# The Fourier half of an attention + FNet kernel: sequence transform first with stored operand pieces, feature transform second

## The chip, the cores and the metric

One core of one Trainium2 chip runs the whole program; the other cores are idle. The metric is the device time of one execution in microseconds (us); the time of a kernel is the median of its runs. Engines: PE (TensorE, matmuls), DVE (VectorE), ACT (ScalarE), POOL (GpSimd) and SP (SyncE, which here issues nearly all DMA transfers).

## What is computed

Two independent halves with S = 2048 rows, D = 1024 columns, all in float32. Half A is full attention with 32 heads of width 32 and an output projection; half B mixes x with Fourier matrices along both axes and keeps the real part. The two outputs stand side by side.

```python
def _A_ref(x, wqkv, wo):
    B, S, D = x.shape
    H = 32; Dh = D // H
    qkv = (x @ wqkv).reshape(B, S, 3, H, Dh).transpose(2, 0, 3, 1, 4)
    q, k, v = qkv[0], qkv[1], qkv[2]
    p = softmax(einsum("bhqd,bhkd->bhqk", q, k) * Dh ** -0.5)
    o = einsum("bhqk,bhkd->bhqd", p, v)
    return o.transpose(0, 2, 1, 3).reshape(B, S, D) @ wo

def _B_ref(x, dft_seq_re, dft_seq_im, dft_hid_re, dft_hid_im):
    a = einsum("bsd,ed->bse", x, dft_hid_re)
    b = einsum("bsd,ed->bse", x, dft_hid_im)
    y = einsum("ts,bse->bte", dft_seq_re, a) - einsum("ts,bse->bte", dft_seq_im, b)
    return y
```

The real part is therefore Cr x Wr' - Ci x Wi', with C the sequence matrices (2048 x 2048) and W the feature matrices (1024 x 1024). The products may be taken from either side.

## The kernel before

**Matmuls.** Every dense product (qkv, the two Fourier steps, the projection) is done to more than the precision of one pass: an operand piece is a raw float32 tile that is split into a rounded high half and a low half (raw minus high), and each 128x128 by 128x512 chunk costs three matmuls, high·high, low·high and high·low (`group`, L404). Each such product also goes through one level of a seven-multiplication scheme: seven products of sums of quadrants in place of eight (`ORDER`), so that operands are often sums of two or three quadrants, and results are gathered from several products (`gather`, L950 to L982). What is stationary is called a piece (four chunks, tiles `h` and `l`, rings HR and LR of four each); what is moving lies in slots (`moving`, one slot holds both halves).

**Making an operand.** `fetch` loads a raw quadrant (L453, tile `raw`, a ring of six), loads a second one if there is a sum (L462, tile `g`), adds them on POOL or DVE (L469) and stores sums that are needed again (L478). `halves` casts the high half on DVE (L491) or on ACT (L489, where `spare` allows it) and subtracts the low half on POOL or DVE (L494). SP issues in its own order; a transfer whose ring place is not yet free holds back all that follow.

**Attention.** Three streams: S, the scores (L1278, tile `psS`, pairs of matmuls), whose row maxima DVE takes (L1284) and whose exponentials' sums ACT takes (L1287); T, the transposed scores with the maxima as two extra rows of `qs` (L1400, tile `psT`), exponentials by ACT into `pt` (L1404); V, the product with v (L1419, batches of 20, 20 and 24 matmuls a quarter wide). Before the first T of a head the maxima go from DVE to DRAM (L1325, `m_d`) and come back into `qs` (L1326). A head's result is scaled by `rt` (L1448) and stored to `o_d` (L1450). 

**Order of the work.** A planner in the program (`Plan`) imitates the engines with assumed costs and writes a fixed order for PE, ACT, DVE, POOL and SP. The chunks of the dense products are a list of fills in program order: qkv, `dense1`, `dense2`, `project`. The planner starts a fill where no attention matmul is ready or where fills are behind their share of the attention work; so the two Fourier steps lie between the matmuls of the heads. `rank` sets which of the ready operations of an engine goes first. After the last head come the rest of the Fourier fills and then the projection, which reads `o_d` and the weights `wo`: its slots 20 to 27 are gated by all stores of `o_d` (`behind`), its raw tiles are a ring of six of their own, and its products run in the order 1, 7, 2, 6, 5, 3, 4, 96 matmuls each.

**Fourier half before.** `dense1` multiplies x (stationary pieces, from `xb`) by the two feature matrices at once (moving, from `wd`): 7 products x 16 groups of 4 chunks, results to DRAM (`ab_d`). `dense2` multiplies pieces of the sequence matrices (stationary, from `ct`) with `ab_d` (moving): for each of two halves m of the inner dimension 7 products x 8 groups of 8 chunks, the first half's results to `y_d` and added at the end of the second (tile `c`).

Of the kernel before, what the change touches and what calls it, by code (L numbers as in the profile page):

```python
# [220 lines left out]
def kernel(  # L221
# [26 lines left out]
    ab_d = [[[dram.tile([P, NB], F32, name=f"ab_d{m}_{e}_{k}") for k in range(NS)] for e in range(2)] for m in range(2)]  # L248

    s1_d = [[dram.tile([P, 4, P], F32, name=f"s1_d{x}_{i}") for i in range(8)] for x in (5, 6)]  # L250
    t1_d = [[dram.tile([P, NB], F32, name=f"t1_d{x}_{n}") for n in range(8)] for x in (5, 6)]
# [5 lines left out]
    u3_d = [[dram.tile([P, NB], F32, name=f"u3_d{i}_{m}") for m in range(2)] for i in range(8)]  # L257
    s2_d = [[[dram.tile([P, 4, P], F32, name=f"s2_d{x}_{i}_{k}") for k in range(4)] for i in range(8)] for x in (5, 6)]
    t2_d = [[[dram.tile([P, NB], F32, name=f"t2_d{x}_{m}_{k}") for k in range(8)] for m in range(2)] for x in (5, 6)]
    y_d = [[dram.tile([P, NB], F32, name=f"y_d{i}_{e}") for e in range(2)] for i in range(NS)]  # L260
# [83 lines left out]

    MM, PV, SWITCH, TINY = 0.2275, 0.853, 0.40, 0.17
# [16 lines left out]
    FILL = 3 * (7 * 24 * 4 + 7 * 16 * 4 + 7 * 8 * 16 + 2 * 8 * 4)  # L362
# [559 lines left out]
    ORDER = (1, 2, 5, 6, 7, 3, 4)  # L922

# [6 lines left out]

    def gather(what, X, Y, u3, to, wrote, part=None, split=False):

# [13 lines left out]
        def finish(ps, last):  # L946
# [63 lines left out]
            if what in (2, 3):  # L1010
                return put(X.at, [X.users], X.last, ALU.add, to, wrote, part)
            if Y is None:
                return put(lambda: got["c"], [cusers], cload, ALU.subtract, to, wrote, part)
            return put(Y.at, [Y.users], Y.last, ALU.subtract, to, wrote, part)
# [3 lines left out]
    ab_st = [[[[] for _ in range(NS)] for _ in range(2)] for _ in range(2)]  # L1018

    def dense1():  # L1020
        s1, t1 = ({5: [[] for _ in range(8)], 6: [[] for _ in range(8)]} for _ in range(2))
        u3 = [[[], []] for _ in range(8)]

        def a_terms(p, i):
            q = lambda r, k: xb[8 * r + i, :, 4 * k : 4 * k + 4, :]
            return {
                1: [(1, q(0, 0), [])], 2: [(1, q(0, 1), [])], 4: [(1, q(1, 1), [])],
                5: [(1, q(1, 0), []), (1, q(1, 1), [])],
                6: [(1, s1_d[0][i], s1[5][i]), (-1, q(0, 0), [])],
                7: [(1, q(0, 0), []), (-1, q(1, 0), [])],  # L1030
                3: [(1, q(0, 1), []), (-1, s1_d[1][i], s1[6][i])],
            }[p]

        def b_terms(p, n):
            m, c = divmod(n, 4)
            q = lambda k, e: wd[m, 4 * k + c, :, e * NB : e * NB + NB]
            return {
                1: [(1, q(0, 0), [])], 2: [(1, q(1, 0), [])], 3: [(1, q(1, 1), [])],
                5: [(1, q(0, 1), []), (-1, q(0, 0), [])],
                6: [(1, q(1, 1), []), (-1, t1_d[0][n], t1[5][n])],  # L1040
                7: [(1, q(1, 1), []), (-1, q(0, 1), [])],
                4: [(1, t1_d[1][n], t1[6][n]), (-1, q(1, 0), [])],
            }[p]

        def load_b(x, n):
            p = ORDER[x]
            B[x][n] = moving((8 * x + n) % 12, b_terms(p, n), (t1_d[p - 5][n], t1[p][n]) if p in (5, 6) else None)

        B = [[None] * 8 for _ in ORDER]
        for n in range(4):  # L1050
            load_b(0, n)
        X = {}
        for x, p in enumerate(ORDER):
            for i in range(8):
                a = piece(a_terms(p, i), (s1_d[p - 5][i], s1[p][i]) if p in (5, 6) else None)
                if i == 0:
                    for n in range(4, 8):
                        load_b(x, n)
                if p == 1:
                    X[i] = accs(SUMS[i])  # L1060
                for m in range(2):
                    h = DONE.get(p)
                    to = ab_d[m][h[1]][8 * h[0] + i] if h else None
                    group(
                        ((chunk(a, c), (B[x][4 * m + c], whole)) for c in range(4)), 4,
                        gather(p, X[i][m], None, (u3_d[i][m], u3[i][m]), to, ab_st[m][h[1]][8 * h[0] + i] if h else None),
                    )
                if i % 2:
                    load_b(x + 1, i // 2) if x < 6 else load_ab(0, i // 2)

    AB = {}
    t2 = {x: [[[] for _ in range(8)] for _ in range(2)] for x in (5, 6)}

    def load_ab(step, k):
        m, x = divmod(step, 7)
        p = ORDER[x]

        q = lambda r, e: (ab_d[m][1 - e][8 * r + k], ab_st[m][1 - e][8 * r + k])
        terms = {
            1: [(1, *q(0, 0))], 2: [(1, *q(1, 0))], 3: [(1, *q(1, 1))],  # L1080
            5: [(1, *q(0, 1)), (-1, *q(0, 0))],
            6: [(1, *q(1, 1)), (-1, t2_d[0][m][k], t2[5][m][k])],
            7: [(1, *q(1, 1)), (-1, *q(0, 1))],
            4: [(1, t2_d[1][m][k], t2[6][m][k]), (-1, *q(1, 0))],
        }[p]
        AB[step, k] = moving((8 * (7 + step) + k) % 12, terms, (t2_d[p - 5][m][k], t2[p][m][k]) if p in (5, 6) else None)

    def dense2():

        y_st = [[[], []] for _ in range(NS)]  # L1090
        for m in range(2):
            s2 = {x: [[[], []] for _ in range(8)] for x in (5, 6)}

            def a_terms(p, i, k0):
                q = lambda r, k: ct[8 * r + i, :, 16 * m + 8 * k + k0 : 16 * m + 8 * k + k0 + 4, :]
                return {
                    1: [(1, q(0, 0), [])], 2: [(1, q(0, 1), [])], 4: [(1, q(1, 1), [])],
                    5: [(1, q(1, 0), []), (1, q(1, 1), [])],
                    6: [(1, s2_d[0][i][2 * m + k0 // 4], s2[5][i][k0 // 4]), (-1, q(0, 0), [])],
                    7: [(1, q(0, 0), []), (-1, q(1, 0), [])],  # L1100
                    3: [(1, q(0, 1), []), (-1, s2_d[1][i][2 * m + k0 // 4], s2[6][i][k0 // 4])],
                }[p]

            X = {}
            for x, p in enumerate(ORDER):
                step = 7 * m + x
                for i in range(8):
                    if p in (1, 5) and i % 2 == 0:
                        X[p, i // 2] = accs(SUMS[(0 if p == 1 else 4) + i // 2])

                    def terms():
                        for k in range(0, 8, 4):
                            if i == 0 and k:
                                for c in range(4, 8):
                                    load_ab(step, c)
# [12 lines left out]
                    if step < 13 and i % 2:  # L1128
                        load_ab(step + 1, i // 2)
# [461 lines left out]
```

## Time and profile before

| | before |
|---|---|
| median of 3 runs | 2942.41 us (2941.58 to 2943.34) |
| span of the profiled execution | 2940.5 us |
| busy: PE, DVE, ACT, POOL | 100%, 79%, 77%, 28% |
| granted TensorE clock | 1.00 throughout |
| moved by DMA | 562.78 MB, mean 191 GB/s |
| share of the 16 DMA engines taken by SP's queue | 58.8% |
| matmul records | 14920 |

The span runs from the first to the last instruction of one execution; the device time of a run is about 2 us more. The page cuts the span into 40 slices; a windows view does the same for chosen stretches, and gives for every engine the busy time and the instructions, then the granted clock, the share of the DMA engines and what they moved. Matmuls are pipelined: one that is shown as 0.39 us long starts 0.23 us after the one before it. A PV matmul has two records, so a batch of 24 is shown as x48.

### The profile page before, as it was taken

The page shows a single profiled execution, that of the slowest core. Times are in us where ns is not written, and L with a number is a line of the kernel's source. Part 1 is how long each engine was busy: PE and PEld are TensorE (multiplying, and loading weights), DVE is VectorE, ACT ScalarE, POOL GpSimd, SP SyncE. Part 2 cuts the span into 40 slices and gives each one's busy share as a digit, 9 for nine tenths or more (in the row PEclk, how much of TensorE's full clock was granted, in tenths as well). Part 3 has the DMA queues.
Part 4 walks back from the last instruction along what each step waited for, and adds up shares of the span by engine and source line. Part 5 has one row for each costly group of instructions (what it writes and reads, how often), then busy time and mean ns, then how long its engine had stood idle before and what let it go on. Part 6 is the DMA issues. An engine that isn't in the chain of part 4 may idle for free.

```text
span 2940.5 us, 45511 instructions
## 1 busy us (share of the span) xinstructions
PE 2934.3 (100%) x14920; PEld 2146.0 (73%) x14920; DVE 2328.2 (79%) x3196; ACT 2278.3 (77%) x4317; POOL 833.3 (28%) x650
## 2 busy tenths in 40 slices
PE   9999999999999999999999999999999999999999
PEld 8887777777777767777777777777777777677787
DVE  7679888788877987777777898888777888887585
ACT  5347888888888888888888888888888888887431
POOL 2324335132212332241111332333112333343042
PEclk9999999999999999999999999999999999999999
DMA  9965668676525653664425775554334677555663
GB/s 372 348 229 194 195 191 292 194 251 225 191 93 164 226 189 111 205 206 147 150 84 161 237 224 189 171 167 151 110 110 139 220 238 222 168 178 176 211 209 118
DMA packets 378455, 562.78 MB, mean 191 GB/s; under 512 B 111183, under 2 KB 111439, under 8 KB 378095
## 3 DMA queue, kind: packets, MB, share of 16 engines
q1 hardware_dynamic: 378076, 559.75, 58.8%
q8 instruction: 120, 1.97, 0.3%
q14 instruction: 115, 0.93, 0.1%
q10 hardware_dynamic: 144, 0.13, 0.0%
HBM read 385.65 MB, written 174.08 MB: 190 GB/s over the span
## 4 chain that ended last, share of the span: by engine, by line
PE 98%; DMA 1%; DVE 1%; ACT 0%; issue 0%; POOL 0%; SPq 0%; DVEq 0%; POOLq 0%; ACTq 0%
PE pd L404 44%; PE psT L1400 16%; PE psS L1278 16%; PE pd L1419 15%; PE psT L404 7%; DVE negm L1284 0%; DMA raw<-in_xb 0%; DMA g<-in_ct 0%; DMA raw<-ab_d 0%; ACT psS L1287 0%; DMA g<-in_xb 0%; DMA slot<-in_xw 0%; DVE l L494 0%; POOL raw L469 0%; DVE raw L469 0%
## 5 line engine op out<-in xcount | busy, mean ns | idle before, releaser
L1404 ACT ACTIVATE pt<-psT 128x512 f32<-128x512 f32 x2048 | 1193.8, 671 | 347.3 <-PE psT L1400 345.5
L1284 DVE TENSOR_REDUCE negm<-psS 128x1 f32<-128x1024 f32 x1024 | 1241.2, 1220 | 211.5 <-PE psS L1278 204.4
L1287 ACT ACTIVATE psS<-psS,negm 128x1024 f32<-128x1024 f32 x1024 | 1188.9, 1161 | 70.9 <-DVE negm L1284 66.8
L404 PE MATMUL pd<-slot,h 128*128 128x512 f32 x3400 | 1155.7, 389 | 0.0
L1400 PE MATMUL psT<-qs,ks 128*128 128x512 f32 x2048 | 802.3, 395 | 0.0
L404 PEld LDWEIGHTS pd<-slot,h 128*128 128x128 f32 x3400 | 638.3, 188 | 132.6
L404 PE MATMUL pd<-slot,l 128*128 128x512 f32 x1700 | 661.3, 389 | 0.0
L1400 PEld LDWEIGHTS psT<-qs,ks 128*128 128x128 f32 x2048 | 381.4, 188 | 157.3 <-issue 63.7
L1278 PE MATMUL psS<-ks,qs 128*128 128x512 f32 x1552 | 472.1, 390 | 0.7 <-ACT psS L1287 0.6
L1419 PE MATMUL pd<-pt,vt 128*32 128x512 f32 x4096 | 459.3, 594 | 0.0
L494 POOL TENSOR_TENSOR l<-raw,h 128x512 fp32r<-128x512 f32 x143 | 184.7, 1292 | 707.8 <-PE psT L1400 366.5
L404 PEld LDWEIGHTS pd<-slot,l 128*128 128x128 f32 x1700 | 319.1, 188 | 67.3 <-issue 0.8
L494 POOL TENSOR_TENSOR slot<-raw,slot 128x512 fp32r<-128x512 f32 x162 | 208.4, 1291 | 535.5 <-DVE slot L491 197.6
L469 POOL TENSOR_TENSOR raw<-raw,g 128x512 f32<-128x512 f32 x186 | 241.9, 1306 | 397.4 <-DMA raw<-t_d 48.9
L1278 PEld LDWEIGHTS psS<-ks,qs 128*128 128x128 f32 x1552 | 290.7, 188 | 62.2 <-ACT psS L1287 3.3
L1419 PEld LDWEIGHTS pd<-pt,vt 128*32 128x32 f32 x4096 | 123.3, 110 | 282.6 <-issue 265.7
L1287 ACT ACTIVATION_READ_ACCUMULATOR psS<-psS,negm 128x1 f32 x1024 | 285.9, 279 | 0.0
L404 PE MATMUL pd<-slot,slot 128*128 128x512 f32 x768 | 191.9, 389 | 0.0
L1432 DVE TENSOR_TENSOR ot<-ot,pd 128x512 f32<-128x512 f32 x64 | 44.0, 687 | 155.1 <-PE pd L1419 154.9
L404 PEld LDWEIGHTS pd<-slot,slot 128*128 128x128 f32 x768 | 144.2, 188 | 30.0
L491 DVE CAST h<-raw 128x512 fp32r<-128x512 f32 x321 | 147.5, 461 | 17.4 <-PE pd L404 14.2
L1278 PE MATMUL psS<-ks,qx 128*128 128x512 f32 x496 | 149.1, 391 | 0.0
(130 smaller groups left out, 1858.4 us busy)
## 6 DMA issues: line engine op xcount, KB each, us to landing
raw<-in_ct SPq DMA_DIRECT2D x192, 256.0 KB
qk_d<-e SPq DMA_DIRECT2D x52, 512.0 KB
qs<-qk_d SPq DMA_DIRECT2D x128, 192.0 KB
ks<-qk_d SPq DMA_DIRECT2D x128, 192.0 KB
raw<-ab_d SPq DMA_DIRECT2D x96, 256.0 KB
g<-in_ct SPq DMA_DIRECT2D x96, 256.0 KB
c<-u_d SPq DMA_DIRECT2D x88, 256.0 KB
s_d<-raw SPq DMA_DIRECT2D x80, 256.0 KB
```

Of the source, the lines that this page charges most:

```text
L404: nc.tensor.matmul(box["ps"], a[1]((a[0].hi, a[0].lo)[u]()), b[1]((b[0].hi, b[0].lo)[v]()), start=k == 0, stop=k == n - 1)
L469: (nc.gpsimd if e == "POOL" else nc.vector).tensor_tensor(out=dest(), in0=dest() if a is None else a.get(), in1=other["q"] if "q" in other ...
L491: nc.vector.tensor_copy(hi(), raw())
L494: (nc.gpsimd if e == "POOL" else nc.vector).tensor_tensor(out=lo(), in0=raw(), in1=f(hi()), op=ALU.subtract)
L1278: nc.tensor.matmul(p[:, i * NB : i * NB + NB], (QX[0] if own else QS[h % 2])[:, qt * P : qt * P + P], KS[h % 2][:, c * 1024 + i * NB : c * ...
L1284: nc.vector.tensor_reduce(out=ST["negm"][:, c, qt : qt + 1], in_=box["p"], axis=AX.X, op=ALU.max, negate=True)
L1287: nc.scalar.activation(box["p"], box["p"], AF.Exp, bias=ST["negm"][:, c, qt : qt + 1], accum_out=ST["sums"][:, c, qt : qt + 1])
L1400: nc.tensor.matmul(box["p"], KS[h % 2][:, t * P : t * P + P], QS[h % 2][:, j * NB : j * NB + NB], start=True, stop=True)
L1404: nc.scalar.activation(box["t"], box["p"], AF.Exp)
L1419: nc.tensor.matmul(po["p"][j * DH : j * DH + DH, :], VT[h][:, k, :], box["t"], start=(k == t0), stop=(k == t), tile_position=(0, j * DH),)
L1432: nc.vector.tensor_tensor(out=po["o"], in0=po["o"], in1=po["p"], op=ALU.add)
```

## The change

The Fourier half is computed from the other side. `dense1` multiplies the transposed x (stationary pieces of `xb`, in a new layout) by the sequence matrices (moving, from `ct`), once for the real (r = 0) and once for the imaginary part (r = 1): 14 products (`outers`), each of 2 halves n x 4 groups of 8 chunks. The pieces of x are the same for r = 0 and 1 and for n = 0 and 1: each is made once, its two halves are stored to DRAM as they are (`ha_d`, `keep_a`, L1235), and every later use loads them straight into the tiles `h` and `l` (`again`, L1388) without a raw tile, cast or subtraction. Results go to `g_d` in rows of 128 numbers (L1120). `dense2` multiplies pieces of `g_d` (stationary) by the feature matrices (moving, from `wd`), 7 products x 8 groups of 8 chunks, and writes the output at once: `ab_d`, `y_d` and the loads of `c` from `y_d` are gone. `spare` is set in `dense1`, so ACT may cast pieces there. With `TWO = set()` the branches for a second level (`gather2`, `aside`, `load_r`, `load_b`) are never taken. Lines of the other functions move (fill matmul L404 to L408, fetch L453 and L462 to L457 and L466, T L1400 to L1787, S L1278 to L1665, PV L1419 to L1806, `m_d` L1325 and L1326 to L1712 and L1713, `o_d` L1450 to L1837).

```diff
+    ORDER = (1, 2, 5, 6, 7, 3, 4)
+    TWO = set()
...
+    def keep_a(a, pp, p, i):
+        rank = seq()
+        kept_a[pp, p, i] = [op("SP", ISSUE, lambda k=k, t=t: nc.sync.dma_start(ha_d[pp][p][i][:, k * NB : k * NB + NB], f(t()).rearrange("p t c -> p (t c)")), [made], [u], rank, 256)
+                            for k, (t, made, u) in enumerate(zip((a.hi, a.lo), a.made, a.users.lists))]
...
     def dense1():
+        spare[0] = True
+        outers = [(r, pp) for r in range(2) for pp in ORDER]
...
+        def load_l(g, c):
+            o, n = divmod(g, 2)
+            if o < 14 and outers[o] not in TWO:
+                terms, store = b_terms(*outers[o], c // 4, n, c % 4)
+                L[o, n, c] = moving((8 * g + c) % NR, terms, store)
...
+        def again(pp, p, i):
...
+            for k, (key, ring) in enumerate(zip("hl", (HR, LR))):
+                d, st = ha_d[pp][p][i][:, k * NB : k * NB + NB], kept_a[pp, p, i][k % len(kept_a[pp, p, i])]
+                old, users = ring.take()
...
+                made.append(op("SP", ISSUE, lambda d=d, get=get: nc.sync.dma_start(f(get()).rearrange("p t c -> p (t c)"), d), old + [st], [users], rank, 256, ring))
+                lists.append(users)
+            return Piece(*tiles, made, Both(*lists))
...
+                for n in range(2):
+                    for m in range(4):
...
+                                if (pp, key, i) in kept_a:
+                                    a = again(pp, key, i)
+                                else:
+                                    a = piece([a_outer(pp, m, k)])
+                                    keep_a(a, pp, key, i)
...
+                        group(terms(), 8, gather1(pp, *place_of((r1, n), i), XY[1][pos] if r in PURE else None, XY[5][pos] if r in PURE and pp in (5, 7, 4) else None))
...
     def dense2():
...
-            for x, p in enumerate(ORDER):
-                step = 7 * m + x
-                for i in range(8):
...
+                to = out[t * P : t * P + P, D + e * NB : D + e * NB + NB]
+                group(terms(), 8, gather(p, X[1, i // 2][i % 2], X[5, i // 2][i % 2] if p not in (1, 2) else None, None, to, [], flip=True))
...
-        "xb": c(B_x[0].reshape(NS, P, NC, P).transpose(0, 3, 2, 1)),
+        "xb": c(B_x[0].reshape(4, 4, P, NC, P).transpose(3, 0, 2, 1, 4)),
-        "ct": c(np.stack([cr, ci]).reshape(2, NS, P, NS, P).transpose(1, 4, 0, 3, 2).reshape(NS, P, 2 * NS, P)),
+        "ct": c(np.stack([cr.T, ci.T]).reshape(2, NS, P, S)),
```

Counted over the whole order: the fill matmuls stay 6720, T and S 2048 each, PV 96 batches. SP issues 2781 transfers in place of 2445; new among them are 168 loads each of `h` and `l` from `ha_d`, 56 stores each of them and 64 stores to `g_d`; gone are 96 loads of `raw` from `ab_d`, 64 stores to it, 32 stores to `y_d` and 32 loads back. DVE has 3019 instructions in place of 3198, ACT 3374 in place of 3296, POOL 652 in place of 655. The casts to high halves stay 629, the pieces and moving tiles that are made stay 448.

The planner lays the rest out anew. First place, the start of a head (here head 8, counted from 0): PE before, with the last PV batch of the head ahead, this head's first T (`qs_553`) and the next head's first S (`qx`):

```order
L1278 MATMUL psS<-ks_2502,qx 128x512 x2
L1419 MATMUL pd<-pt,vt 32x512 x24
L1400 MATMUL psT<-qs_553,ks_554 128x512 x2
L1278 MATMUL psS<-ks_2502,qx 128x512 x4
L404 MATMUL pd<-slot_8765,h 128x512
```

PE now, from the same PV batch:

```order
L1806 MATMUL pd<-pt,vt 32x512 x24
L1665 MATMUL psS<-ks_2610,qx 128x512 x4
L408 MATMUL pd<-slot_9378,h 128x512
L408 MATMUL pd<-slot_9378,l 128x512
L408 MATMUL pd<-slot_9378,h 128x512
L408 MATMUL pd<-slot_9409,h 128x512
L408 MATMUL pd<-slot_9409,l 128x512
L408 MATMUL pd<-slot_9409,h 128x512
L408 MATMUL pd<-slot_9764,h 128x512
L408 MATMUL pd<-slot_9764,l 128x512
L408 MATMUL pd<-slot_9764,h 128x512
L1787 MATMUL psT<-qs_661,ks_662 128x512 x2
```

The first T moves behind four S and nine fills; heads 10 and 29 have the same shape with six and eight fills. SP before, around the store and the load of this head's maxima (`m_d_168`):

```order
L453 DMA raw<-in_wd 128x512
L478 DMA t_d_0_281<-raw 128x512
L462 DMA g<-in_wd 128x512
L305 DMA ks_2502<-qk_d_2_84 96x512
L453 DMA raw<-in_xb 128x512 x2
L1325 DMA m_d_168<-lt 4x32x32
L453 DMA raw<-in_wd 128x512
L1326 DMA qs_553<-m_d_168 2x2048
```

SP now, around the same two:

```order
L307 DMA ks_2610<-qk_d_3_85 96x512
L307 DMA qs_2609<-qk_d_0_78 96x512
L307 DMA qs_2609<-qk_d_1_79 96x512
L307 DMA qs_2609<-qk_d_2_80 96x512
L1712 DMA m_d_168<-lt 4x32x32
L307 DMA qs_2609<-qk_d_3_81 96x512
L1828 DMA qs_2609<-z_d 2x2048
L1235 DMA ha_d_1_1_284<-h 128x512
L1235 DMA ha_d_2_1_286<-h 128x512
L1750 DMA r_d_136<-ll 4x32x32
L457 DMA raw<-in_xb 128x512
L1713 DMA qs_661<-m_d_168 2x2048
```

Six transfers instead of one now stand between the store and its load; ahead of the first row shown stand ten more of 96x512 or 128x512 (a load of keys, four stores to `ha_d`, loads of `ct` and `xb`). Second place, the passage from the last head to the projection. On PE 104 fill matmuls stood between the last PV batch and the projection's first; now 65 do. SP before, from the loads of `wo` for product 1 (`raw`), through those of `o_d` for it, with loads for kept sums (`s`, `g`) and output stores between:

```order
L453 DMA raw<-in_wo 128x512 x4
L453 DMA raw<-o_d_193 128x512
L453 DMA raw<-o_d_194 128x512
L453 DMA s_0_0_30216<-o_d_193 128x512
L982 DMA out<-e 128x512
L942 DMA c<-y_d_1_540 128x512
L462 DMA g<-o_d_193 128x512
L453 DMA s_0_1_30248<-o_d_194 128x512
L453 DMA raw<-o_d_195 128x512
L453 DMA raw<-o_d_196 128x512
```

SP now, from the first of the same `o_d` loads:

```order
L457 DMA raw<-o_d_193 128x512
L457 DMA raw<-o_d_194 128x512
L457 DMA s_0_0_30671<-o_d_193 128x512
L466 DMA g<-o_d_193 128x512
L984 DMA out<-e 128x512
L457 DMA s_0_1_30689<-o_d_194 128x512
L457 DMA s_0_2_30694<-o_d_195 128x512
L457 DMA s_0_3_30699<-o_d_196 128x512
L457 DMA s_1_0_30708<-o_d_193 128x512
L457 DMA s_1_1_30716<-o_d_194 128x512
L457 DMA s_1_2_30726<-o_d_195 128x512
L457 DMA raw<-o_d_195 128x512
```

Six loads for kept sums now stand between the output store and the third load of `o_d` (`o_d_195`), where one stood before.

499 lines of the change are left out of this document (400 added, 99 removed).

## Prediction

> **What bounds the kernel now.** The page of the profile comes first, then PE's waits, then busy time by stretches.
>
> ```profile
> span 2940.5 us, 45511 instructions
> PE 2934.3 (100%) x14920; PEld 2146.0 (73%) x14920; DVE 2328.2 (79%) x3196; ACT 2278.3 (77%) x4317; POOL 833.3 (28%) x650
> ```
>
> PE is busy for 2934.3 of 2940.5 us; no other compute engine is over 79%. The waits that the trace can name on PE are these three:
>
> ```profile
> PE pd L369 <- DVE c L367: 1.5, 1, 1.5
> PE psS L1278 <- ACT psS L1287: 0.6, 3, 0.2
> PE psT L404 <- ACT slot L489: 0.2, 1, 0.2
> ```
>
> The columns are the total, the times and the longest, in us: 2.3 us in all, 1.5 of it at the very start. The kernel is bound by the number of matmuls, and the static order leaves PE hardly a gap. The stretches (for each engine busy us and instructions, then clock, share and rate of the DMA engines) show where other resources come near their limit:
>
> ```profile
> core 0: us, PE busy (x) PEld busy (x) DVE busy (x) ACT busy (x) POOL busy (x), PEclk, DMA share, GB/s
> 0.00:100.00 100.00, 98.39 (x426) 80.77 (x427) 74.15 (x110) 47.62 (x80) 30.41 (x27) 1.00 1.00 372
> 470.00:548.00 78.00, 78.00 (x409) 55.88 (x408) 68.61 (x95) 66.67 (x129) 33.14 (x26) 1.00 0.88 288
> 787.00:865.00 78.00, 78.00 (x408) 55.88 (x408) 57.01 (x74) 67.10 (x130) 3.87 (x3) 1.00 0.24 68
> 942.00:1024.00 82.00, 81.82 (x423) 58.36 (x422) 70.48 (x97) 69.25 (x132) 23.16 (x18) 1.00 0.65 216
> 1024.00:1105.00 81.00, 80.84 (x419) 57.48 (x418) 66.05 (x91) 67.25 (x131) 26.75 (x21) 1.00 0.55 179
> 2765.00:2770.00 5.00, 5.00 (x24) 4.14 (x23) 3.08 (x6) 0.88 (x2) 0.00 (x0) 1.00 0.92 278
> 2770.00:2775.00 5.00, 5.00 (x24) 4.14 (x23) 4.47 (x8) 2.90 (x5) 1.06 (x1) 1.00 1.02 370
> 2775.00:2800.00 25.00, 25.00 (x112) 20.70 (x111) 21.39 (x31) 9.41 (x16) 8.00 (x7) 1.00 1.04 390
> ```
>
> The five long rows after the header are the start and four heads (from one store of maxima to the next), the last three the passage from attention to the projection. The granted clock is 1.00 throughout, so it is no term. The DMA engines are full in two places only, the first 100 us and that passage. The chain that ended last tells the passage on PE (start, us, what):
>
> ```profile
> 2755.19 5.29 PE pd L1419 x48
> 2760.48 2.07 PE pd L404 x8
> 2762.54 5.45 PE psT L404 x24
> 2768.00 10.88 PE pd L404 x48
> 2778.88 8.16 PE psT L404 x36
> ```
>
> The last PV batch ends at 2760.48. 24 fill matmuls take 5.45 us (0.227 us each), and 48, in groups of other sizes, take 10.88: the same price, so how chunks are bundled into groups costs PE nothing. 2760.48 plus the 104 matmuls that the order puts before the projection (104 x 0.227 = 23.6 us) gives 2784.1 for its first matmul: these 23.6 us hide the fetching of its operands.
>
> **The change, part by part.** *Matmuls.* PE's order has 6720 fills, 2048 T, 2048 S and 96 PV batches before and after: nothing saved, nothing added. The largest that any other edit can give back is the 2.3 us of named waits; of these the 1.5 us at the start lies in the unchanged part, so at most 0.8 us. I put it at 0.
>
> *Work of the other engines.* VectorE has 179 instructions fewer (3198 to 3019 in the order), ScalarE 78 more, of which 35 cast pieces. All have room: in the head of 942 to 1024 us VectorE has 70 of 82 us busy, ScalarE 69. Casts are as many as before (629) and pieces made are as many (448), so nothing large moves here: 0 on the path. The stores in 512-byte rows (64, for g_d) are not in the trace of before; they are issued behind the evacuation and read tens of us later. I put them at 0 on the path, their DMA time inside the next term.
>
> *More transfers in attention.* SP issues 2781 transfers for 2445. In place of raw pieces that two engines then split, 168 pieces come in two transfers each, straight into PE's operands, and the ring holds four. Where the order packs them densest, between the stores of maxima of heads 9 and 10, SP has 111 transfers (27.0 MB), for 74 (17.5 MB) before, which is 0.65 of the DMA engines in the row from 942 us. The price of more: the head from 787 us moved 78 x 68 GB/s = 5.3 MB in 0.24 x 78 = 18.7 us of DMA time, that from 470 us 22.5 MB in 68.6 us, so 2.9 us for each further MB. 9.5 MB more than 17.7 are 27.2 MB, or 68.6 + 4.7 x 2.9 = 82 us of DMA time in a head of some 80 us. SP thus falls 2 to 4 us behind, and the next head (24.6 MB, 75 us) hands little of it back. A piece in a ring of four is loaded when the piece three before it starts, 36 fill matmuls earlier; PE runs about half fills in a head, so this lead is near 15 us, against some 5 us to land in a full queue (below). It hides most. Bounds: 0, since the head from 470 us ran PE without a gap at 0.88; 6, if the lag of 4 us and a load put just ahead of its first use (one in the order, near the eighteenth head) both come through. I take **1.5 us**, nearer to the row of 470 us.
>
> [...]
>
> *The start of a head.* The first transposed scores need the row maxima to go to DRAM (L1325) and back (L1326). At head 8:
>
> ```profile
> 865.07 0.52 SPq L1325 DMA_DIRECT2D m_d<-lt  x1
> 865.64 0.46 SPq L453 DMA_DIRECT2D raw<-in_wd  x1
> 867.04 0.26 SPq L1326 DMA_DIRECT2D qs<-m_d  x1
> ```
>
> ```profile
> 874.86 0.74 PE L1400 MATMUL psT<-qs,ks 128*128 128x512 f32 x2
> ```
>
> Before, the queue is nearly empty (0.24 of the DMA engines in the row from 787 us): 1.97 us from the store to the load, which has 7.8 us until it is needed. In the changed order some ten large transfers stand ahead of the store and six between it and its load. The order itself now puts four S and nine fills (13 x 0.227 = 3.0 us) ahead of the head's first T, so the need moves to 877.8. A transfer of 0.262 MB takes 0.67 us at 390 GB/s; eight in flight take 5.4. The store then lands at 865.1 + 2.0 + 5.4 = 872.5, and the load, with five of those six still ahead of it, 2.0 + 3.4 later: 877.9, just late; with half of the queue, early. Three heads (8, 10 and 29) have this shape. Bounds: 0, and 5 if the load too meets eight transfers in each of the three (3 x 1.7). I take **1.5 us**.
>
> *The passage to the projection.* This is the term I trust most. 65 matmuls instead of 104 now follow the last PV: 14.7 us of cover instead of 23.6, and the chain behind the cover, which starts with that head's store, does not shorten as much. Before, it ran like this on SP, then ScalarE and VectorE:
>
> ```profile
> 2762.04 0.32 SPq L1450 DMA_DIRECT2D o_d<-ot  x1
> 2764.23 0.34 SPq L982 DMA_DIRECT2D out<-e  x1
> 2765.14 1.83 SPq L453 DMA_DIRECT2D raw<-in_wo  x4
> 2767.01 0.91 SPq L453 DMA_DIRECT2D raw<-o_d  x2
> 2769.69 0.34 SPq L982 DMA_DIRECT2D out<-e  x1
> 2772.54 1.52 SPq L453 DMA_DIRECT2D raw<-o_d  x3
> ```
>
> ```profile
> 2769.05 1.33 ACT L489 ACTIVATE slot<-raw 128x512 fp32r<-128x512 f32 x2 [14.78 <-DMA raw<-in_wo]
> 2777.38 1.31 ACT L489 ACTIVATE slot<-raw 128x512 fp32r<-128x512 f32 x2 [3.27 <-DMA raw<-o_d]
> ```
>
> ```profile
> 2771.82 1.89 DVE L494 TENSOR_TENSOR slot<-raw,slot 128x512 fp32r<-128x512 f32 x3
> ```
>
> Six raw tiles hold the four loads of wo and two of o_d; the third of o_d waits for a low half to free one (2771.82 + 0.69 = 2772.5, and it issues at 2772.54) and reaches its cast 4.84 us later. The projection needs that cast at its seventh matmul, 2784.1 + 1.4 = 2785.5: 7.5 us to spare. After, with zero at the end of the last PV: SP stops at its second store of `out` until the group that ends with the 41st matmul is evacuated (41 x 0.227 + 0.69 = 10.0); then come six loads for kept sums at some 0.47, which stood behind the third load before, so that this issues at 10.1 + 0.4 + 2.8 = 13.3, lands and is cast by 13.3 + 4.84 + 0.63 = 18.8. The seventh matmul is due at 14.7 + 1.4 = 16.1. PE waits 2.7 us, and about 0.3 more for the low halves (0.69 each on VectorE): 3.0. Bounds: 2.1 with the 3.9 us from the wo load (2765.14) to its cast, 5 with eight transfers ahead.
>
> Product 7 follows 96 matmuls later. Its last sums need some 36 transfers after the tenth us, 36 x 0.67 = 24 us, done near 36.5; PE needs them at 14.7 + 3.0 + 21.8 = 39.5, but VectorE's order puts three of the low halves behind the copy of PE's last group of product 1: 0.5 us (0 to 2.5). Together **3.5 us**.
>
> *Sum.* 1.5 + 1.5 + 3.5 = 6.5 us on the span of 2940.5 gives 2947.0. The median of the runs is 2942.41, 1.9 above that span: **2949.0 us**.
>
> **Rivals.** (a) *Not slower.* Place: the passage. If the third load of o_d lands 2.7 us earlier than I reckon, because SP is not held at the second store of `out` (its evacuation depends on how VectorE's casts fall), the 14.7 us are cover enough; from arrival at 16.1 on PE waits for nothing. [...] For: the matmul count is equal, and PE has 2.3 us of waits in 2940. Against: the hold is there in before, 2767.01 to 2769.69. Time 2942.4 + 0 to 3: 2942 to 2946.
>
> (b) *DMA engines bind in heads 9 to 12.* If each of the loads that PE now takes straight from DRAM shares the lag that ends at head 10, and the heads' starts their upper bound, 6 + 5 + 3.5 = 14.5 us: 2957. For: 82 us of DMA time in 80. Against: 15 us of lead.
>
> (c) *Faster.* It would need more than 5.9 us, and the named waits hold 2.3. Only a cheaper matmul could bring it, such as fewer switches between banks; the equal price of 24 and 48 above speaks against it. Time 2936.
>
> **How the numbers follow.** A measurement of this kernel can tell about 0.2% (5.9 us) from no change. Chances: my forecast 0.55 (2945 to 2954), (a) 0.25, (b) 0.17, (c) 0.03. Of the forecast's 0.55 about 0.14 lies under 2948.3. So faster 0.03, same 0.39, slower 0.58. The range 2942 to 2960 leaves out (c), the lower end of (a), and the far end of (b), where its parts add to other mishaps.
>
> **What would show it.** Right: at the first projection matmuls a wait of about 3 us for ScalarE's cast of a slot, released by raw<-o_d; the third o_d load some 13 us after the last PV; waits of PE on h or l loads and on the maxima only in heads 8 to 12 and near 29, each under 2 us; a DMA share over 0.95 between the maxima of heads 9 and 10. Wrong: PE's waits still near 2 us in all; or a new wait in a stage that I hold equal, such as a moving tile of dense1 or a copy of g_d that comes late.

## The result and the profile after

The changed kernel takes 2955.95 us (median of 4 runs, 2953.44 to 2958.55), the kernel before 2942.19 us beside it: a ratio of 1.0046 (95% interval 1.0032 to 1.006), 13.8 us slower. The forecast was 2949.0 us. The profile is of the shortest of the four runs, 2953.44 us.

The page of the changed kernel's profile, and under it PE's waits (total, times, longest, in us):

```profile
span 2951.6 us, 46087 instructions
PE 2939.8 (100%) x14920; PEld 2148.0 (73%) x14920; DVE 2244.0 (76%) x3017; ACT 2318.7 (79%) x4395; POOL 829.5 (28%) x647
```

```profile
PE psT L408 <- ACT slot L493: 3.0, 1, 3.0
PE psT L408 <- POOL slot L498: 1.9, 2, 1.3
PE pd L373 <- DVE c L371: 1.5, 1, 1.5
PE psT L1787 <- DMA qs<-m_d: 1.2, 3, 0.9
```

The matmuls are as many as before, and PE is busy 5.5 us longer for the same work. That alone says that some of them ran slowly. The named waits are 7.6 us in place of 2.3. The span grew by 11.1 us, so about half of it is in no wait. Where it is, the stretches show (busy us and instructions of each engine, then clock, DMA share, rate):

```profile
core 0: us, PE busy (x) PEld busy (x) DVE busy (x) ACT busy (x) POOL busy (x), PEclk, DMA share, GB/s
944.00:1031.00 87.00, 87.00 (x448) 63.25 (x446) 71.84 (x101) 75.97 (x145) 37.91 (x30) 1.00 0.93 317
1031.00:1110.00 79.00, 79.00 (x411) 56.28 (x410) 64.84 (x87) 67.48 (x132) 30.04 (x24) 1.00 0.95 317
2788.00:2790.00 2.00, 0.66 (x2) 0.22 (x2) 2.00 (x4) 0.63 (x1) 0.00 (x0) 1.00 1.02 355
2790.00:2792.00 2.00, 0.33 (x1) 0.29 (x1) 0.57 (x2) 0.74 (x2) 0.00 (x0) 0.83 1.05 405
2792.00:2794.00 2.00, 2.00 (x5) 1.31 (x5) 1.43 (x3) 0.52 (x1) 0.00 (x0) 0.50 1.05 399
2794.00:2796.00 2.00, 2.00 (x7) 1.52 (x6) 1.36 (x3) 1.70 (x4) 0.00 (x0) 0.50 1.05 402
2796.00:2798.00 2.00, 2.00 (x6) 1.61 (x5) 1.43 (x3) 1.07 (x2) 0.43 (x1) 0.50 1.06 390
2798.00:2800.00 2.00, 2.00 (x10) 1.55 (x10) 0.73 (x2) 0.00 (x0) 0.85 (x1) 0.96 1.05 388
```

PE stands still around 2788 to 2791 us, ahead of the projection; then the granted clock falls to 0.50 for some 7 us, and a matmul starts every 0.43 us instead of 0.227. The stall is paid for twice. In steps of half a microsecond the clock's deficit adds up to 3.42 us. In other runs below it is 0, 1.71, 3.42, 5.12 or 6.83 us: always near a multiple of 1.71, which is what 3.41 us at half clock take. In the 3.41 us before the clock fell, at 2791.31, PE stood still for 2.85 us.

How the stall comes about is in the chain that ended last (start, us, what):

```profile
2780.98 3.42 PE psT L408 x15
2784.40 0.02 issue
2784.42 0.64 ACT slot L493
2785.06 0.02 issue
2785.08 0.70 DVE slot L498
2785.79 5.18 DMA raw<-o_d
2790.97 0.02 issue
2790.99 0.64 ACT slot L493
2791.63 0.04 issue
2791.67 3.23 PE psT L408 x6
```

It begins on PE. PE's last fills release a slot, ScalarE casts a tile of wo into it, VectorE subtracts, that frees a raw tile, the third o_d load starts, and its cast lets PE go on. PE waits for a chain that PE's own last fills held up. ScalarE's row shows where that begins:

```profile
2784.42 2.88 ACT L493 ACTIVATE slot<-raw 128x512 fp32r<-128x512 f32 x5 [8.21 <-PE psT L408]
```

Before the change ScalarE's first cast of wo waited for the load of wo. Now it waits 8.21 us for PE. This was in the code: the last product of `dense2` used to take slots (8 x 20 + k) mod 12 = 4 to 11; with the new offset, (8 x 6 + k + 8) mod 12, it holds 8 to 11 and 0 to 3, and the projection's first product wants its weights in 0 to 3.

The third o_d load was late for a second reason, SP's order (start, duration, transfers):

```profile
2782.12 3.30 SPq L457 DMA_DIRECT2D s<-o_d  x6
2785.79 0.97 SPq L457 DMA_DIRECT2D raw<-o_d  x2
```

The six loads for kept sums end at 2785.42, and the subtraction that frees the raw tile at 2785.78. So the held slots by themselves put this load off by 0.4 us; most of the delay is the six loads ahead of it, as the prediction had it. But that order is laid out for these slots too: where the slots are free (e10 below), one such load stands ahead of it instead of six.

The span's 11.1 us split at the last PV batch. The end of attention, measured from PE's first matmul, came 10.9 us later; 39 fills that now lie ahead of it are 8.84 us of that, so the **heads lost 2.1 us**. From there to PE's last matmul, corrected for the same 39 fills, the **passage lost 9.0 us**: 3.4 half clock, the rest standing still.

### The profile page after: what moved, and what is told of

It reads as the page before. It is cut to its first block, busy times and chain, and to the rows that moved or that the text cites. A ratio compares the mean times of both kernels' runs of the same rounds, so it can differ in the third digit from the quotient of the medians.

```text
span 2951.6 us, 46087 instructions
## 1 busy us (share of the span) xinstructions
PE 2939.8 (100%) x14920; PEld 2148.0 (73%) x14920; DVE 2244.0 (76%) x3017; ACT 2318.7 (79%) x4395; POOL 829.5 (28%) x647
## 4 chain that ended last, share of the span: by engine, by line
PE 98%; DMA 1%; DVE 1%; ACT 0%; issue 0%; SPq 0%; POOL 0%; DVEq 0%; POOLq 0%; ACTq 0%
PE pd L408 45%; PE psT L1787 16%; PE psS L1665 16%; PE pd L1806 15%; PE psT L408 6%; DMA qs<-m_d 0%; DMA m_d<-lt 0%; DVE negm L1671 0%; DMA raw<-in_xb 0%; DMA raw<-o_d 0%; PE pd L373 0%; ACT psS L1674 0%; SPq L307 0%; POOL slot L498 0%; DVE l L498 0%
## 5 line engine op out<-in xcount | busy, mean ns | idle before, releaser
L408 PE MATMUL pd<-slot,h 128*128 128x512 f32 x3416 | 1160.9, 389 | 0.0
L1787 PE MATMUL psT<-qs,ks 128*128 128x512 f32 x2048 | 802.0, 395 | 1.3 <-DMA qs<-m_d 1.2
L408 PEld LDWEIGHTS pd<-slot,h 128*128 128x128 f32 x3416 | 641.6, 188 | 133.9 <-ACT acc L792 0.4
L408 PE MATMUL pd<-slot,l 128*128 128x512 f32 x1708 | 664.4, 389 | 0.0
L498 POOL TENSOR_TENSOR slot<-raw,slot 128x512 fp32r<-128x512 f32 x243 | 312.0, 1292 | 892.0 <-DVE slot L495 416.6
L1787 PEld LDWEIGHTS psT<-qs,ks 128*128 128x128 f32 x2048 | 381.6, 188 | 156.5 <-issue 65.4
L1665 PE MATMUL psS<-ks,qs 128*128 128x512 f32 x1552 | 471.7, 390 | 0.3
L1806 PE MATMUL pd<-pt,vt 128*32 128x512 f32 x4096 | 459.3, 594 | 0.0
L408 PEld LDWEIGHTS pd<-slot,l 128*128 128x128 f32 x1708 | 320.6, 188 | 67.5 <-issue 0.8
L1665 PEld LDWEIGHTS psS<-ks,qs 128*128 128x128 f32 x1552 | 290.7, 188 | 61.8 <-ACT psS L1674 2.8
L1806 PEld LDWEIGHTS pd<-pt,vt 128*32 128x32 f32 x4096 | 123.3, 110 | 282.8 <-issue 266.7
L473 POOL TENSOR_TENSOR raw<-raw,g 128x512 f32<-128x512 f32 x170 | 222.0, 1311 | 335.9 <-DMA raw<-in_ct 40.2
L1674 ACT ACTIVATION_READ_ACCUMULATOR psS<-psS,negm 128x1 f32 x1024 | 292.6, 286 | 0.0
L498 POOL TENSOR_TENSOR l<-raw,h 128x512 fp32r<-128x512 f32 x100 | 129.2, 1292 | 455.8 <-PE psT L1787 182.8
L408 PE MATMUL pd<-slot,slot 128*128 128x512 f32 x768 | 193.8, 392 | 0.0
L408 PEld LDWEIGHTS pd<-slot,slot 128*128 128x128 f32 x768 | 145.5, 189 | 30.4
L1665 PE MATMUL psS<-ks,qx 128*128 128x512 f32 x496 | 149.8, 392 | 0.0
L408 PE MATMUL psT<-slot,slot 128*128 128x512 f32 x576 | 138.7, 392 | 4.9 <-ACT slot L493 3.0
```

Source lines behind the costliest of these rows:

```text
L408: nc.tensor.matmul(box["ps"], a[1]((a[0].hi, a[0].lo)[u]()), b[1]((b[0].hi, b[0].lo)[v]()), start=k == 0, stop=k == n - 1)
L473: (nc.gpsimd if e == "POOL" else nc.vector).tensor_tensor(out=dest(), in0=dest() if a is None else a.get(), in1=other["q"] if "q" in other ...
L498: (nc.gpsimd if e == "POOL" else nc.vector).tensor_tensor(out=lo(), in0=raw(), in1=f(hi()), op=ALU.subtract)
L1665: nc.tensor.matmul(p[:, i * NB : i * NB + NB], (QX[0] if own else QS[h % 2])[:, qt * P : qt * P + P], KS[h % 2][:, c * 1024 + i * NB : c * ...
L1674: nc.scalar.activation(box["p"], box["p"], AF.Exp, bias=ST["negm"][:, c, qt : qt + 1], accum_out=ST["sums"][:, c, qt : qt + 1])
L1787: nc.tensor.matmul(box["p"], KS[h % 2][:, t * P : t * P + P], QS[h % 2][:, j * NB : j * NB + NB], start=True, stop=True)
```

## The experiments

Every kernel below was taken apart in the same way, from one profile each. Fills are those behind the last PV batch; "held" means that the slots of the projection's first weights are held by the last Fourier product; clock is the part of the passage's loss that the half clock takes.

| kernel | fills | slots | median us | ratio to before (95%) | heads | passage | clock |
|---|---|---|---|---|---|---|---|
| before | 104 | free | 2942.19 | 1 | 0 | 0 | 0 |
| changed | 65 | held | 2955.95 | 1.0046 (1.0032 to 1.006) | 2.1 | 9.0 | 3.4 |
| e9_after, changed again | 65 | held | 2955.85 | 1.0044 (1.003 to 1.0058) | 7.1 | 7.4 | 1.7 |
| e1_dummy16 | 65 | held | 2957.41 | 1.0047 (1.0035 to 1.006) | 9.9 | 3.0 | 0 |
| e2_dummy8 | 65 | held | 2956.58 | 1.0045 (1.0032 to 1.0057) | 5.9 | 6.6 | 1.7 |
| e3_ring8 | 65 | held | 2959.15 | 1.0052 (1.0038 to 1.0065) | 5.8 | 13.1 | 6.8 |
| e4_cover67 (of before) | 67 | free | 2947.93 | 1.0015 (1.0006 to 1.0024) | 1.6 | 4.0 | 0 |
| e7_nospare | 103 | held | 2958.2 | 1.0052 (1.004 to 1.0065) | 2.5 | 10.2 | 5.1 |
| e6_pooladds | 96 | held | 2952.06 | 1.0034 (1.0022 to 1.0047) | 2.6 | 6.2 | 1.7 |
| e5_remake | 53 | held | 2952.02 | 1.0032 (1.002 to 1.0045) | 1.3 | 8.5 | 3.4 |
| e10_slots | 65 | free | 2952.69 | 1.0035 (1.0022 to 1.0047) | 3.2 | 6.4 | 1.7 |
| e13_before_slots (of before) | 104 | held | 2945.27 | 1.0012 (1.0003 to 1.0021) | -1.1 | 2.9 | 0 |
| e11_slots_pool | 96 | free | 2946.59 | 1.0014 (1.0006 to 1.0023) | 5.8 | 0.3 | 0 |
| e12_noload | 107 | free | 2943.95 | 1.0003 (0.9994 to 1.0012) | 2.2 | 0.0 | 0 |

For e1 and e2 the 3.6 and 1.8 us of added matmuls are not counted as loss. Where the intervals of two ratios overlap, as those of e9 and e10 or of e11 and e12 do, the times alone hardly tell the two kernels apart. The edits, other than those of e1 and e2, also change the static order that the planner lays out.

### Does the gap make the clock fall? (e1_dummy16, e2_dummy8)

In `group`, once, ahead of the projection's first matmul (n = 16 or 8), into the bank that the real matmul then starts afresh:

```diff
                     if k == 0:
                         box["ps"] = bank()
+                        for _ in range(idle_fill.pop() if idle_fill and order is fills and a[0] is late.get("first") else 0):
+                            nc.tensor.matmul(box["ps"], a[1](a[0].hi()), b[1](b[0].hi()), start=True, stop=True)
```

> The changed kernel with 16 extra matmuls that nobody reads, run on PE right ahead of the projection's first one (16 x 0.227 = 3.6 us of added work; the order of every engine is otherwise the same). Theory A (the loss is the wait at the projection, and the half clock that follows it is caused by PE standing idle): PE works through most of the 3.2 us gap, the granted clock stays at 1.00, and the 3.5 us that half speed cost are saved although work was added: about 2952 us against 2956, and the runs lie closer together. Rival B (the clock falls there for another reason, such as the load of the whole passage): the clock falls all the same and the time stays at 2956 or rises to 2959. Rival C (the loss is spread over heads 9 to 12 by crowded DMA engines): no change or slower.

> As the run with 16 extra matmuls, but 8 of them (1.8 us): the longest gap of PE shrinks from 3.2 us to about 1.4 us. Theory A: if the length of the gap decides, the clock stays at 1.00 and the time falls by about 3.5 us to 2952; if any gap will do, the clock falls as before and the time stays near 2956. Rivals B and C: 2956 or more.

Both came out at 2957, no faster. In the passage the first half of theory A held: with 16, PE's gap shrinks to under 1 us and the clock stays at 1.00, and the passage is 2.4 us shorter than in the profile of the changed kernel (0.8 shorter than in its repeat), with 3.6 us of useless work put in. With 8, a gap of 2.4 us between two starts is left, and the clock still falls, by one quantum. But the heads of these executions lost 9.9 and 5.9 us, not 2.1, and that swallowed it. Theory A had called the whole loss a matter of the passage; in these executions that was wrong. In e1 the largest piece is at 1135 us:

```profile
1128.81 6.29 DMA g<-in_xb
1135.10 0.03 issue
1135.13 0.02 DVEq L476
1135.15 0.04 issue
1135.20 0.69 DVE raw L476
1135.89 1.14 DVE negm L1675
1137.03 0.02 issue
1137.06 0.02 ACTq L1678
1137.07 0.04 issue
1137.12 1.21 ACT psS L1678 x2
1138.33 0.04 issue
1138.37 0.73 PE psS L1669 x2
```

A second term lands 6.29 us after its issue. VectorE's addition stands waiting for it, the row maxima stand behind the addition, ScalarE's exponentials behind the maxima, and PE's next S behind those: PE waits 2.8 us for a fill's operand that no matmul needed yet. Here too the clock then falls (stretches of e1):

```profile
1138.00:1140.00 2.00, 1.63 (x7) 1.16 (x8) 1.61 (x2) 2.00 (x5) 0.00 (x0) 0.98 0.86 280
1140.00:1142.00 2.00, 2.00 (x6) 1.57 (x5) 0.80 (x2) 2.00 (x5) 0.07 (x1) 0.50 0.62 225
1142.00:1144.00 2.00, 2.00 (x9) 1.16 (x11) 1.23 (x1) 1.30 (x4) 1.21 (x1) 0.67 0.37 137
```

### Room for the loads, and the short cover alone (e3_ring8, e4_cover67)

```diff
-        where[0] = (Ring(6), Ring(5), lambda shape, name, n: op_pool().tile(shape, F32, name=name, tag=name, bufs=n), over)
+        where[0] = (Ring(8), Ring(3), lambda shape, name, n: op_pool().tile(shape, F32, name=name, tag=name, bufs=n), over)
```

> The changed kernel with eight raw tiles for the projection's operands in place of six (and three tiles for second terms in place of five, for room): the third and fourth loads of o_d no longer wait for a low half, and the six loads for kept sums fall behind them. The cover stays 65 matmuls. Theory A: the third o_d load is issued near 8 us after the last PV, lands before 16 us, PE does not wait at product 1 and the clock stays at 1.00: 4.3 + 3.5 us less, near 2948 us, and the waits at product 7 (1.5 us) stay or grow by 1 to 2 us with the smaller ring for second terms. Rival C: 2956, since the heads are untouched. Rival D (the cover of 65 is too short for any order of the loads): the wait only moves to product 7, 2953 to 2956.

Slower, 2959.15 us. The order did put the third and fourth o_d load right behind the second, and the wait at product 1 shrank to short pieces, which still made the clock fall; at product 7 PE now stood still for 3.1 us and again for 1.6 us, and the clock fell once more, for three quanta. The chain there runs through VectorE's sums; that the smaller ring for second terms made them late was not tested by itself. Rival D describes the place of the wait, not the time.

In the kernel before:

```diff
-    RES = 400
+    RES = 294
```

> The kernel before with the planner's reserve of fills cut from 400 to 294, so that only 67 fill matmuls instead of 104 follow the last PV; no part of the change is in it. Its order has two loads for kept sums ahead of the third o_d load, not six. Theory A: this shows what the short cover alone costs: the third o_d cast comes near 17.6 us after the last PV, its matmul is due at 16.6, so a wait of 1 to 2 us, too short for the clock to fall: 2943 to 2945 us against 2942. Rival D: a stall as in the changed kernel, with the half clock: 2949 to 2951. Rival C: 2942, no change.

2947.93 us: the short cover costs 4.0 us in the passage without any of the change, 1.7 at product 1 and 2.3 at product 7, and the clock stays. So it is not nothing (rival C) and not the 9 us of rival D; theory A expected half of what came, since I had left out product 7.

### Which part of the change? (e9_after, e7_nospare, e6_pooladds, e5_remake)

> The changed kernel once more, beside the next three on their chip, as their measure: about 2956 us if the loss is the same everywhere; theory A2 (about 9 us at the projection that are the same in every execution, and a loss in the heads through late transfers that differs between executions, 2 to 8 us) expects the runs to spread over 5 us or more.

The median is the same as on the first chip; the profile splits otherwise (heads 7.1, passage 7.4). PE's waits of e9 that were not there in the first profile are the S matmuls behind late maxima:

```profile
PE psS L1665 <- ACT psS L1674: 5.2, 8, 1.6
```

The runs spread over 3.1 us, less than I expected.

```diff
     def dense1():
-        spare[0] = True
+        spare[0] = False
```

> The changed kernel without one of its lines: ScalarE casts no high halves in the two Fourier steps (as before the change). SP's transfers in heads 7 to 13 stay as many (83 to 106 a head in the densest); the planner's order now leaves 103 fills behind the last PV instead of 65. Theory A2: the 9 us at the projection go, the loss in the heads stays: 2945 to 2949 us against 2956, clock 1.00 at the projection. Rival C (all of the loss comes from the crowded transfers in the heads): 2954 to 2957.

The order has 103 fills behind the last PV, as in before, and the passage lost 10.2 us, more than ever. **Theory A2 falls here in its part on the passage**: restoring the cover does not restore the time. ScalarE's rows in the passage pointed to the reason:

```profile
2784.86 1.31 ACT L493 ACTIVATE slot<-raw 128x512 fp32r<-128x512 f32 x2 [5.58 <-PE psT L408]
```

The casts of wo end with PE's last fills, however many those are, because they hold the slots. More cover only moves the casts back with it; and the order now has SP issue all eight loads for kept sums ahead of the third o_d load, which goes out at 2785.12.

For e6 the additions in the two Fourier steps may only be taken by GpSimd:

```diff
-                      rank, 0, raws if keep is None and last is None else None, other=("DVE", ADD, 20 + rank), two=True)
+                      rank, 0, raws if keep is None and last is None else None, other=None if on_pool[0] else ("DVE", ADD, 20 + rank), two=True)
```

> The changed kernel with the additions of second terms in the two Fourier steps kept on GpSimd (VectorE has 18 of them instead of 138), so that no addition that waits for a late transfer stands ahead of the row maxima on VectorE; transfers as many; 96 fills behind the last PV. Theory A2: PE's waits for ScalarE behind the maxima in the heads go too: 2942 to 2946 us and runs closer together. Rival C2 (late transfers reach PE directly through h, l and the maxima's own way, not through VectorE's queue): the same as the run without ScalarE's casts, 2945 to 2949, with waits in the heads still of several us.

2952.06 us, outside both ranges; the heads lost 2.6 us instead of 7.1, but the passage, which I thought mended by the cover, 6.2. In e5 every use makes its piece anew:

```diff
-                                if (pp, key, i) in kept_a:
+                                if False:
...
-                                    keep_a(a, pp, key, i)
```

> The changed kernel without stored pieces: each use makes the piece of x anew from raw (280 transfers fewer on SP; some 85 instead of 111 in the densest head; 110 more high and 170 more low halves to make). Its order leaves only 53 fills behind the last PV. Theory A2: the loss in the heads shrinks to under 1 us, while the wait at the projection grows by up to 12 x 0.227 = 2.7 us: 2951 to 2957 in all, and the trace tells the two apart. Rival E (the loss in the heads is from the engines' new work and not from transfers): the heads lose as much or more, 2957 to 2962.

2952.02 us, 3.8 less than e9 beside it, although its passage lost 1.1 us more. The heads lost 1.3 us. The head that had a DMA share of 0.93 now has 0.79, with more work on the engines:

```profile
944.00:1031.00 87.00, 87.00 (x459) 62.14 (x461) 72.22 (x105) 76.80 (x148) 40.90 (x32) 1.00 0.79 248
```

So the time points to the transfers of the stored pieces and away from the engines' work (rival E). It is no proof of it: the heads lost 2.1 us in the first profile of the changed kernel, with all these transfers, and 2.2 in e12 below, without them.

### The slots (e10_slots, e13_before_slots, e11_slots_pool, e12_noload)

The same edit in the changed kernel (e10), where it frees the slots, and in the kernel before (e13), where it makes the clash:

```diff
-            1: ([20, 24], 0), 7: ([4, 8], 20), 2: ([0, 4], 24), 6: ([8, 0], 20),
-            5: ([4, 8], 24), 3: ([0, 4], 20), 4: ([8, 0], 24),
+            1: ([20, 24], 4), 7: ([8, 0], 20), 2: ([4, 8], 24), 6: ([0, 4], 20),
+            5: ([8, 0], 24), 3: ([4, 8], 20), 4: ([0, 4], 24),
```

> The changed kernel with the projection's weight tiles of its first product in slots 4 to 7 in place of 0 to 3 (the following products' slots turned round in the same way); cover still 65, transfers the same. Theory F: the wait at the projection comes from slots, since the last product of dense2 now holds slots 8 to 11 and 0 to 3 to its very end, so that the casts of wo, and with them the raw tiles that the third o_d load needs, wait for PE's last fills. Here slots 4 to 7 are free: the casts of wo come 8 to 9 us after the last PV instead of 12.8 to 15, the third o_d load near 10 us, PE waits 1 to 4 us in the passage with the clock at 1.00: 2948 to 2951 us against 2956. Theory A (the cover is too short, the slots do not matter): 2954 to 2956.

> The kernel before with the same edit of the projection's slots and nothing else: its last Fourier product ends in slots 4 to 11, so here the edit makes the clash that the change made. Cover still 104. Theory F: the casts of wo wait for the last fills although the cover is long; PE stops for 3 to 5 us, the clock falls to half, and the time rises by 8 to 11 us to 2950 to 2953. Theory A: 104 fills cover it, 2942 to 2944.

e10: 2952.69 us, 3.2 less than e9, on another chip. With the slots SP's order has changed too: the third o_d load stands behind one load for a kept sum and goes out 11.0 us after the last PV, for 14.4 before the edit. At product 1 the wait is down to 0.4 us, as theory F has it. But PE, now earlier, stands still at product 7 for 4 us, and that costs one quantum of clock. The chain there:

```profile
2809.05 0.60 DVE slot L952
2809.64 1.39 DVE t L473
2811.03 0.28 DVE slot L498
2811.31 0.25 issue
2811.55 0.68 DVE slot L952
2812.23 1.36 DVE t L473
2813.59 0.61 DVE slot L498
2814.21 0.04 issue
2814.25 3.64 PE psT L408 x10
```

VectorE's queue is the next limit: the two additions `t` start while GpSimd is at a subtraction of 1.3 us (from 2809.19 and from 2811.78) and take 1.4 us, where one in the changed kernel's profile, at 2808.66 with GpSimd idle, took 0.68. e13: 2945.27 us, 2.7 over the kernel before. The clash costs, in the predicted direction and place (below, e13's waits), but a third of what I expected, and the clock did not fall. Here too the order follows the slots: the third o_d load stands behind all eight loads for kept sums, at 2779.66 instead of 2772.54.

```profile
PE psT L404 <- ACT slot L489: 1.8, 1, 1.8
PE pd L369 <- DVE c L367: 1.5, 1, 1.5
PE psT L404 <- DVE slot L494: 0.5, 1, 0.5
```

e11 joins e10's edit with e6's, free slots with additions on GpSimd, which leaves 96 fills; e12 adds the edits of e7 and e5 to these, so that ScalarE takes no casts of the Fourier steps and no piece is stored, with 107 fills.

> The changed kernel with free slots for the projection and the additions of the Fourier steps on GpSimd; 96 fills behind the last PV. Theory F with a loss of about 2.5 us in the heads: no wait over 1 us at the projection, clock 1.00, 2944 to 2947 us. Theory A2 without F: 2951 to 2953, as the run with the additions alone.

> The changed kernel with free slots, additions on GpSimd, no high halves on ScalarE in the Fourier steps, and no stored pieces (each is made anew, 280 transfers fewer); 107 fills behind the last PV. If late transfers, the queues that they block and the slots are all of the loss, this is the kernel before with its Fourier half taken in the other order and costs nothing: 2941 to 2944 us, PE's named waits near 3 us. If the other order of the products costs anything of itself, 2946 or more.

e11: 2946.59 us, the passage back to 0.3 us, the clock at 1.00. e12: 2943.95 us, ratio 1.0003 (0.9994 to 1.0012), no measurable difference from before, with these waits in all:

```profile
PE psS L1667 <- ACT psS L1676: 1.9, 2, 1.3
PE pd L373 <- DVE c L371: 1.5, 1, 1.5
```

So no cost of the other order of the products itself shows; the interval leaves room for 3.5 us. The sharpest pair is e6 and e11: with 96 fills in both, the edit of the slots, and the order that follows from it, takes the passage's loss from 6.2 to 0.3 us and 5.5 us off the median. In the passage, free slots with 96 or more fills lose 0 to 0.3 us; held slots with 96 or more 2.9 to 10.2; free slots with 65 or 67 fills 4.0 and 6.4; held with 65, 7.4 and 9.0 (e1 to e3, which change more there, left out). Either fault alone is enough to stop PE, and mending one shows the other. No version beat the kernel before.

## Why the prediction was right and wrong

**Direction and kind: right.** Slower, by a wait at the projection and by late transfers in the heads, with equal matmul work. The wait that it named is there: 3.0 us for ScalarE's cast of a slot released by an o_d load, 2.7 forecast; the third o_d load went out at 2785.79, 14.4 us after the last PV's end (2771.42), for some 13 forecast. The DMA share between the maxima of heads 9 and 10 is 0.93, for over 0.95. The time, 2955.95 us, is above the 2945 to 2954 that the prediction gave its own forecast, and between that and rival (b).

**The passage: 3.5 us forecast, 9.0 measured (7.4 in the repeat).** This is the term that failed in its size. Three things are in the difference. The largest, 3.4 us (1.7 in the repeat), is the half clock, a term put at nothing; the prediction had looked at the clock, seen 1.00 everywhere and closed it as a term. It became one where PE stood still: in the changed kernel for 2.85 of the 3.41 us ahead of the fall. A gap of 2.42 us between starts did it in e2, one of 2.38 us did not in e4. Next, the chain: the waits at product 1 came to 4.0 us for 3.0. The third o_d load went out 1.1 us later than reckoned, 0.7 of it because the store and the loads ahead of it took longer and 0.4 because of the held slots; landing and cast took 0.4 us longer. "The third of o_d waits for a low half to free one" was right, but I took the casts of wo to follow their loads as before, and did not ask who held the slot that they write. Last, product 7 took 1.6 us for 0.5.

**The starts of heads: 1.5 us forecast, 1.2 measured** (0.7 in the repeat), but not at heads 8, 10 and 29; it is a late load of the maxima in three other heads, 11, 19 and 26, so the size is luck. Between PE's starts these three gaps cost 2.2 us, about all that the heads lost in that profile.

**More transfers in attention: 1.5 us forecast, bounds 0 to 6.** PE never waited for a load of `h` or `l`; that picture was wrong. The heads as a whole lost 2.1 us in the first profile, 5.8, 5.9, 7.1 and 9.9 in four others with the same order of the heads, 3.2 in a sixth. What stands behind the larger losses is seen in e1's chain: a transfer that is late holds VectorE's queue, and the maxima stand in it. I had put VectorE's work at zero because it had room. A mean share says nothing on what stands behind a waiting instruction.

**The rivals.** (b), 2957 us, came nearest in time, with the transfers as its cause; the heads hold 2.1 of the span's 11.1 us in the first profile and 7.1 of 14.5 in the repeat. (a) expected the cover to suffice; (c) was rightly excluded.

**Open.** Why the heads of one execution lose 2 us and of another 10 with the same program was not settled. e6's 2.6 and e11's 5.8 us, with additions on GpSimd in both, show that single profiles do not decide it; the medians of e11 and e12 (2946.59 and 2943.95, equal passages) and of e9 and e5 do point at the transfers of the stored pieces, some 2.5 to 4 us, though e12 also takes casts off ScalarE. How much of the slots' price is the held slot and how much the order that the planner makes of it was not told apart. That e13's clash costs 2.9 us and e7's 10.2 was not taken apart further.

## What to carry to other kernels

When a stretch of fills hides a chain, look at both ends of the chain: not only how long the cover is, but whether the cover itself holds a buffer that the chain needs. A stall of TensorE has to be priced with the half clock behind it: here PE stood still for 1.86 to 3.30 us within a step of 3.41 us ahead of each of eleven falls, and each fall cost 1.71 to 5.12 us. And in a static order, an instruction that waits for a transfer is as late as the transfer, and so is everything behind it in its queue, on however idle an engine: in e1 a transfer that landed after 6.29 us held VectorE's queue, and PE waited 2.8 us.

## What the runs showed of the hardware

- After some gaps of PE the granted clock was 0.50, in whole quanta: the loss was 1.71 us (e9, e2, e6, e10, e1 at 1139 us), 3.42 (changed, and e5 in two falls), 5.12 (e7) or 6.83 (e3, in two falls). A matmul of 512 columns then started every 0.43 us, for 0.227.
- A gap of 2.42 us between two starts was followed by the half clock (e2), one of 2.38 us (e4) and one of 2.21 us (e13) were not. The clock's changes lie whole steps of 3.41 us apart: half clock lasts one step (e9, e2, e6, e10, e1, the first falls of e3 and e5), two (6.83 us, changed) or three (10.24 us, e7 and the second fall of e3); the two falls of e3 lie 23.9 us apart, seven steps, those of e5 27.3, eight. In the changed kernel the fall at 2791.31 comes 2785.28 us after the first full clock, 816 steps of 3.413. What went with a fall was PE's standing still within the step ahead of it, counted beyond the 0.227 us of each matmul, in gaps of over 0.55 us between starts: 1.86 us (e1) to 3.30 us (e6) in all eleven. The largest seen in a step at full clock that no fall followed are 1.85 us (e10, one step ahead of its fall) and 1.48 us (changed, from 2815.87). Shorter gaps are left out of the count, so the line is rough. Of e2's gap and the short one behind it 2.36 us lie in one step; where the steps lie in e4 and e13, whose clock did not fall, is not shown.
- 16 matmuls that nobody reads, in front of a wait, kept the clock there at 1.00 (e1): the gap between starts was 0.95 us, for 3.41 in the changed kernel, and the passage lost 3.0 us and 3.6 for the added matmuls, for 9.0 and 7.4 without them.
